# Cosine attention and a gated feed-forward on one core: the order of every engine through the third batch, rewritten

## The chip, the cores and the metric

The kernel runs on one core of one Trainium2 chip. The metric is the device time of one execution in microseconds. Before the change it is 416.95 us, the median of three runs (416.65, 416.95, 417.01).

## The reference, cut to what matters

```python
batch, n_heads, seq, head_dim = (8, 12, 448, 64)          # q, k, v
n_tokens, d_model, d_ff = (3584, 768, 2048)               # w_in, w_out

q_n = q / (np.linalg.norm(q, axis=-1, keepdims=True) + 1e-06)
k_n = k / (np.linalg.norm(k, axis=-1, keepdims=True) + 1e-06)
scores = np.matmul(q_n, k_n.transpose(0, 1, 3, 2)) / tau
attn = np.exp(scores - np.max(scores, axis=-1, keepdims=True))
attn = attn / (np.sum(attn, axis=-1, keepdims=True) + 1e-09)
x = np.matmul(attn, v)              # transposed and reshaped to 3584 x 768
h = x @ w_in
out = (h * np.cos(h)) @ w_out       # 3584 x 768, float32
```

## The kernel before, in words

**Units of work.** Four heads of one batch make a *quad*; there are three quads in a batch and 24 in all. A quad has seven score blocks. One block is four matmuls on TensorE (`scores`, L619), and an exp on ScalarE (L627, and L634 for quad 0) turns it into a tile of `E`. When the seven tiles of a quad are there, `attend` (L646) multiplies them with V. The row sums of `E` come in two ways: quads 0 to 5 use `spread` (L672), whose sums go through a Ln and an Exp of 128x896 elements on ScalarE (L685, L689); later quads use `sums` (L735), on two quads at a time, whose reciprocals are spread by DMA. The product of the two is `xT`.

**Normalization.** For each quad q and k are loaded (L452), squared (L505 on GpSimd or VectorE, L502 on ScalarE), summed (L509, VectorE), inverted by small ScalarE and VectorE instructions (L527 to L545), scaled (L553) and transposed, by TensorE in the first quads (L582, copied out at L590 or L592) and by a DMA later. Quad 0 is split into two pieces along the sequence, here called Q0a and Q0b, K0a and K0b. Its k is only cast (L561), and the scale of k goes into the exp.

**The feed-forward of a batch** has a stage `m1` (L784: eight pairs of blocks of `w_in`, 96 matmuls, with ScalarE L797 and L801 and VectorE L799 and L803 behind each pair) and a stage `m2` (L815: tiles of 128 tokens by 384 outputs, 16 matmuls each, copied out at L827 on VectorE, or on ScalarE where a table says so). Batches of 448 tokens give six, eight, six and eight such tiles in batches 0 to 3. The score blocks of later quads are put between the matmuls of `m2`. Three slots of two PSUM banks go round among score blocks, `spread` and `attend`, so a score block waits for the third one back to be read out. The exp and the sine need different ScalarE tables, so each stage starts with a table load (L424).

**What sets the order.** The kernel is an explicit program: a planner in Python orders the operations of each engine before the program is built, and each engine runs its list strictly in that order.

- The operations are numbered as the source issues them. Up to about number 210 (quads 0 to 2 and the norms of quads 3 and 4) a key, the number plus an entry of `MOVE`, sets the order on every engine's list, DMA issues among them. After that TensorE follows the source, DMA issues of GpSimd keep the order of their keys, and the planner's reckoned times order the rest.
- `VISITS` has a row for each batch: a pair (n, m) takes n entries off the stream of score blocks, spreads and attends, and then m matmuls of `m2`. `LATER` says how many score blocks of a quad go ahead of the attend of the quad before it.
- `ENG` puts single operations on an engine: `s0:16` is the square of q in quad 16 (`s1` of k), `n0` and `n1` the scaling, `x` the product of `attend` and reciprocal, `a` the copy of `attend` out of PSUM, `o:2:1` the copy-out of tile 2, half 1 of `m2`. Defaults are GpSimd for squares, scaling of q and `x`, and VectorE for the copies.
- `TREE` adds tiles of `E` on VectorE ahead of `sums`.
- 143 plus 70 products of the identity (L921, L925) stand in the list of TensorE as filling.

Loads of q and k and the DMA transposes are issued by SyncE (queue q1 of the profile), one piece of k by ScalarE (q10), and V, `w_in` (W1, L474) and `w_out` (W2, L479) by GpSimd (q0). W1(i, h) is half h of the partitions of the columns that `m1`'s pairs 4i to 4i+3 need; W2(i) holds four of the sixteen row blocks.

Numbers that the prediction names: 8 to 15 are the loads of quads 0 to 2, 65 and 66 of quad 3, 146 and 147 of quad 5; 17, 50, 53, 102 load V of quads 0 to 3; 51, 52, 54, 55 load W1(0,0), W1(0,1), W1(1,0), W1(1,1); 103 to 106 load W2(0) to W2(3). 33 squares K0b, 20 squares K0a, 39 and 23 are their sums, 30 is the last step of the inverse norm of Q0, 37 and 38 scale Q0.

Of the kernel before, what the change touches and what calls it, by code (L numbers as in the profile page):

```python
# [28 lines left out]
LATER = {18: -1, 5: 3, 7: -1, 21: -1, 9: 4, 10: -2, 12: 0, 23: 2, 15: -2, 13: -1, 22: 2, 8: 1, 16: 2, 14: 0, 17: -1,  # L29
    19: -1, 20: 0}  # L30
QUADS = [4, 5, 3, 3, 3, 3, 0, 0]
EARLY = [2, 1, 1, 1, 1, 1, 1, 1]
MOVE = {49: 2.0, 100: -6.5, 94: -4.0, 199: 5.5, 198: 3.0, 48: -155.0, 123: 23.0, 33: -18.5, 21: -15.0, 149: -9.5, 143:
# [17 lines left out]
TREE = {12: 3, 11: 0, 13: 0, 16: 4, 14: 6, 15: 6, 17: 4, 18: 2, 19: 0, 23: 6, 20: 6, 22: 5, 21: 6}  # L51
# [1156 lines left out]
```

## Time and profile before

| what | value |
|---|---|
| median of the runs | 416.95 us |
| the profiled execution, its own time | 417.37 us |
| its span, first to last instruction | 415.6 us |
| TensorE busy | 406.9 us (98%) |
| ScalarE busy | 313.7 us (75%) |
| VectorE busy | 306.6 us (74%) |
| GpSimd busy | 199.6 us (48%) |
| granted TensorE clock | 1.00 |

All times inside the execution are counted from the first instruction. PE is TensorE, ACT ScalarE, DVE VectorE, POOL GpSimd, SP SyncE. An instruction's busy time on PE begins before its predecessor's ends, so that the distance between two starts is what one costs.

### The profile page before, as it was taken

What the parts mean: (1) busy time and instruction counts of PE and PEld (TensorE: products, weight loads), DVE (VectorE), ACT (ScalarE), POOL (GpSimd) and SP (SyncE); (2) the same over time, 40 slices, a digit from 0 to 9 for tenths busy, and PEclk for the clock granted to TensorE, in tenths of its full rate; (3) what the DMA queues carried; (4) which work ended last, traced back from release to release, by engine and by line L of the source; (5) the groups of instructions that cost most, each with busy time, mean ns of one, the idle gap of its engine ahead of it and who ended that gap; (6) DMA issues with size and microseconds to landing.
All of it is one profiled execution on the core that took longest, in us unless ns stands there. A gap on an engine that the chain in (4) does not pass through costs nothing.

```text
span 415.6 us, 8581 instructions
## 1 busy us (share of the span) xinstructions
PE 406.9 (98%) x3600; PEld 217.5 (52%) x3601; DVE 306.6 (74%) x368; ACT 313.7 (75%) x417; POOL 199.6 (48%) x132
## 2 busy tenths in 40 slices
PE   7999999999999999999999999999999999999996
PEld 6674544445554455454555555454555555555563
DVE  4958997879853669963899899964988479836931
ACT  5998889988888987878878667889886667715700
POOL 3866329793386862688715495088504050030000
PEclk9999999999999999999999999999999999999999
DMA  8999999986099999199939689299803350071033
GB/s 267 231 244 209 236 225 275 217 180 152 4 205 168 262 236 237 40 177 244 188 113 176 132 181 219 33 162 211 178 2 82 77 108 22 1 165 39 0 77 76
DMA packets 71399, 62.83 MB, mean 151 GB/s; under 512 B 40512, under 2 KB 66240, under 8 KB 71360
## 3 DMA queue, kind: packets, MB, share of 16 engines
q1 hardware_dynamic: 60688, 50.09, 52.3%
q0 software_dynamic: 10240, 11.80, 17.6%
q8 instruction: 28, 0.46, 0.5%
q10 hardware_dynamic: 432, 0.39, 0.3%
q14 instruction: 11, 0.09, 0.1%
HBM read 45.61 MB, written 11.01 MB: 136 GB/s over the span
## 4 chain that ended last, share of the span: by engine, by line
PE 88%; ACT 8%; DVE 1%; DMA 1%; issue 0%; SPq 0%; DVEq 0%
PE PS L815 35%; PE PS L784 35%; PE PS L619 8%; PE PS L646 6%; ACT E L627 5%; PE PS L735 2%; PE PS L672 1%; DMA Kf<-in_k_dram 1%; ACT E L634 1%; ACT ar L689 1%; ACT ar L685 1%; PE PS L582 0%; DVE n L509 0%; DVE AVs L659 0%; DVE Qn L553 0%
## 5 line engine op out<-in xcount | busy, mean ns | idle before, releaser
L815 PE MATMUL PS<-W,gT 128*128 128x384 bf16 (+2 forms) x895 | 156.4, 327 | 0.1
L627 ACT ACTIVATE E<-PS 128x896 f16<-128x896 f32 x161 | 137.0, 917 | 21.8 <-PE PS L619 21.2
L784 PE MATMUL PS<-xT,W 128*128 128x448 bf16 x768 | 147.0, 352 | 0.0
L815 PEld LDWEIGHTS PS<-W,gT 128*128 128x128 bf16 x896 | 83.2, 98 | 69.1 <-issue 15.2
L784 PEld LDWEIGHTS PS<-xT,W 128*128 128x128 bf16 x768 | 74.7, 98 | 70.0 <-issue 0.4
L797 ACT ACTIVATE ar<-PS 128x896 int32<-128x896 f32 x64 | 58.2, 911 | 32.1 <-PE PS L784 31.4
L799 DVE SCALAR_TENSOR_TENSOR ar<-ar,PS 128x896 f32<-128x896 int32 x64 | 69.0, 1084 | 17.9 <-ACT ar L797 17.7
L803 DVE TENSOR_TENSOR gT<-PS,ar 128x896 bf16<-128x896 f32 x64 | 69.3, 1088 | 4.9 <-ACT ar L801 4.3
L801 ACT ACTIVATE ar<-ar 128x896 f32<-128x896 f32 x64 | 60.5, 947 | 16.0 <-DVE ar L799 15.3
L762 POOL TENSOR_TENSOR xT<-AVs,R 128x896 bf16<-128x896 f32 x17 | 37.9, 2231 | 57.4 <-DMA R<-Zs 57.4
L827 DVE COPY osb<-PS 128x384 f32<-128x384 f32 (+2 forms) x56 | 31.1, 554 | 41.6 <-PE PS L815 40.7
L505 POOL TENSOR_TENSOR sqq<-Qf 128x896 bf16<-128x896 f32 x21 | 35.3, 1680 | 44.4 <-DVE n L509 35.1
L619 PE MATMUL PS<-qT,kT 64*64 64x448 bf16 x672 | 51.0, 360 | 2.1 <-ACT E L627 1.2
L553 POOL TENSOR_TENSOR Qn<-Qf,rr 128x896 bf16<-128x896 f32 x20 | 37.9, 1897 | 29.7 <-DVE rr L545 25.7
L722 DVE TENSOR_TENSOR E<-E 128x1792 f16<-128x1792 f16 (+2 forms) x26 | 36.5, 1403 | 4.7 <-PE PS L646 4.5
L646 PE MATMUL PS<-E,Vb 64*64 64x448 f16 x672 | 37.7, 350 | 0.0
L505 POOL TENSOR_TENSOR sqk<-Kf 128x896 bf16<-128x896 f32 x17 | 30.5, 1797 | 13.6 <-DVE n L509 10.7
L553 POOL TENSOR_TENSOR Kn<-Kf,rr 128x896 bf16<-128x896 f32 x17 | 31.2, 1835 | 6.0 <-DVE Qn L553 3.6
L659 DVE COPY AVs<-PS 128x896 f32<-128x896 f32 x21 | 22.8, 1087 | 11.7 <-PE PS L646 11.5
L619 PEld LDWEIGHTS PS<-qT,kT 64*64 64x64 bf16 x672 | 16.3, 105 | 28.0 <-issue 11.3
L509 DVE TENSOR_REDUCE n<-sqq 128x14 f32<-128x896 bf16 (+2 forms) x23 | 23.7, 1035 | 6.8 <-POOL sqq L505 6.0
L646 PEld LDWEIGHTS PS<-E,Vb 64*64 64x64 bf16 x672 | 20.0, 107 | 11.8 <-ACT E L627 0.9
(57 smaller groups left out, 232.8 us busy)
## 6 DMA issues: line engine op xcount, KB each, us to landing
out_dram<-osb SPq DMA_DIRECT2D x54, 192.0 KB, 3.0
Qf<-in_q_dram SPq DMA_DIRECT2D x23, 448.0 KB, 5.1
Kf<-in_k_dram SPq DMA_DIRECT2D x23, 448.0 KB, 5.1
R<-Zs SPq DMA_DIRECT2D x72, 112.0 KB, 3.0
Vb<-in_v_dram POOLq DMA_DIRECT2D x24, 224.0 KB, 5.2
W<-in_moe_w_in_dram POOLq DMA_DIRECT2D x4, 768.0 KB, 17.3
W<-in_moe_w_out_dram POOLq DMA_DIRECT2D x4, 768.0 KB, 25.1
qT<-Qn SPq DMA_TRANSPOSE x20, 4.3
```

The lines of the kernel that those rows point to most:

```text
L505: op(eng, (1.68 if eng == "pool" else 1.05) * n, lambda e: e.tensor_tensor(dst, src, src, ALU.mult), r=cut(nm + "f", s, part), w=own, afte ...
L553: lambda e: e.tensor_tensor(n[0].ap()[:, j0:j1].rearrange("p j r d -> p r j d"), f[s].ap()[:, :, j0:j1], rb, ALU.mult),
L619: ins = e.matmul(bank(bs + r, S, 64 * a, 64 * a + 64), kT[u].ap()[64 * r:64 * r + 64, j, a, :], qT[u].ap()[64 * r:64 * r + 64, :, a, :], s ...
L627: act("exp", 0.81, lambda e: e.activation(E.ap()[:, es], two(bs), ACT.Exp, bias=SHIFT, scale=INV_TAU), r=pair(bs), w=[("E", es)], chain="E")
L646: ins = e.matmul(bank(bk + a, S, 64 * r, 64 * r + 64), Vb[vs].ap()[64 * a:64 * a + 64, r, j, :], E.ap()[64 * a:64 * a + 64, es, r, :], sta ...
L762: op(eng, 2.04 if eng == "pool" else 1.05, lambda e, u=u, sl=sl, b=b, c0=c0: e.tensor_tensor(xT[b % 2].ap()[:, c0:c0 + 2, :], AVs[sl].ap() ...
L784: ins = e.matmul(bank(bk + i2), W1.ap()[:, i, 128 * nb:128 * nb + 128], xT[c % 2].ap()[:, i, :], start=(i == 0), stop=(i == NKC - 1))
L797: op("act", 0.815, lambda e: e.activation(ar[s].ap().bitcast(I32), two(bk), ACT.Identity, bias=0.25, scale=INV2PI), r=bs, w=[("ar", s)], a ...
L799: op("dve", 1.005, lambda e: e.scalar_tensor_tensor(ar[s].ap(), ar[s].ap().bitcast(I32), -2.0 * math.pi, two(bk), ALU.mult, ALU.add), r=bs ...
L801: act("sin", 0.86, lambda e: e.activation(ar[s].ap(), ar[s].ap(), ACT.Sin, bias=GUARD * math.pi / 2.0, scale=GUARD), r=[("ar", s)], w=[("a ...
L803: op("dve", 1.01, lambda e: e.tensor_tensor(gT.ap()[:, 2 * pr:2 * pr + 2, col:col + S], two(bk), ar[s].ap(), ALU.mult), r=bs + [("ar", s)] ...
L815: ins = e.matmul(bank(bk, x1 - x0), gT.ap()[:, f, col:col + 128], W2.ap()[:, f, x0:x1], start=(f == 0), stop=(f == NNB - 1))
```

## The change

Only tables change. Rows 0 to 3 of `VISITS`, and `LATER` for quads 7 and 9, give another interleaving of score blocks and `m2`; the number of pieces and of changes between kinds of matmul stays nearly the same. `MOVE` is written anew for all operations from 7 to 210, so every list has a new order up to the first `m1`. In `ENG` nine copy-outs (`o`) and two `a` go from VectorE to ScalarE, the squares of q in quads 16 and 17 from GpSimd to ScalarE, and four steps (`s1:15`, `n0:16`, `x:10`, `x:13`) from GpSimd to VectorE; the other new entries name the engine that the default gives already. `TREE` of quad 12 becomes 0: three additions less on VectorE.

```diff
 VISITS = [
-    [(0, 25), (3, 12), (3, 11), (3, 3), (3, 5), (3, 12), (3, 10), (3, 4), (3, 4), (3, 0), (3, 4), (3, 5), (1, 1)],
-    [(0, 20), (3, 11), (3, 13), (3, 13), (3, 0), (3, 15), (3, 11), (3, 8), (6, 0), (3, 16), (2, 11), (4, 4), (2, 6),
-        (2, 0)],
-    [(0, 26), (2, 11), (3, 0), (2, 20), (4, 11), (3, 9), (2, 10), (5, 0), (3, 2)],
-    [(0, 21), (3, 9), (3, 11), (3, 8), (2, 8), (4, 26), (4, 17), (2, 12), (3, 11)],
+    [(0, 24), (3, 13), (3, 11), (2, 4), (7, 12), (3, 11), (3, 3), (3, 5), (1, 3), (6, 5), (2, 3), (1, 7)],
+    [(0, 24), (2, 0), (1, 8), (3, 14), (3, 7), (1, 3), (3, 0), (3, 19), (3, 7), (2, 10), (6, 0), (3, 16), (2, 12), (5,
+        4), (3, 7)],
+    [(0, 26), (2, 11), (3, 0), (2, 20), (4, 8), (3, 8), (2, 12), (5, 0), (3, 2)],
+    [(0, 19), (3, 11), (3, 13), (3, 6), (2, 9), (4, 27), (5, 16), (1, 11), (3, 11)],
...
-LATER = {18: -1, 5: 3, 7: -1, 21: -1, 9: 4, 10: -2, 12: 0, 23: 2, 15: -2, 13: -1, 22: 2, 8: 1, 16: 2, 14: 0, 17: -1,
-    19: -1, 20: 0}
+LATER = {18: -1, 5: 3, 7: 0, 21: -1, 9: 5, 10: -2, 12: 0, 23: 2, 15: -2, 13: -1, 22: 2, 8: 1, 16: 2, 14: 0, 17: -1,
+    19: -1, 20: 0, 3: 0, 4: 0, 11: 0}
...
-MOVE = {49: 2.0, 100: -6.5, 94: -4.0, 199: 5.5, 198: 3.0, 48: -155.0, 123: 23.0, 33: -18.5, 21: -15.0, 149: -9.5, 143:
...
+MOVE = {7: -2.38, 8: -8.0, 9: -5.4, 10: -2.8, 11: -11.0, 12: -1.2, 13: 1.4, 14: 31.581, 15: 6.21, 16: 19.154, 17:
+    25.294, 18: 3.48, 19: 10.468, 20: 14.944, 21: 4.754, 22: 11.03, 23: 16.217, 24: 17.411, 25: 18.979, 26: 16.779,
+    27: 11.389, 28: 11.997, 29: 12.605, 30: 13.213, 31: 12.933, 32: 13.541, 33: -0.798, 34: 17.841, 35: 18.449, 36:
+    10.261, 37: 11.707, 38: 8.007, 39: -3.107, 40: 13.147, 41: 14.715, 42: 9.689, 43: 10.915, 44: 0.653, 45: 9.169,
+    46: 9.777, 47: 39.345, 48: -29.13, 49: 3.307, 50: -48.2, 51: 11.387, 52: 14.527, 53: 17.667, 54: 61.079, 55:
+    51.199, 56: 2.583, 57: 4.043, 58: 1.783, 59: 7.263, 60: -10.417, 61: 8.983, 62: -4.257, 63: -34.404, 64: -0.137,
+    65: -11.283, 66: -24.019, 67: 2.281, 68: 5.811, 69: -7.459, 70: 6.385, 71: -5.355, 72: -0.517, 73: 0.091, 74:
...
+    94: -8.921, 95: -8.511, 96: -3.211, 97: -4.781, 98: -3.213, 99: 3.461, 100: 1.459, 101: -9.621, 102: 39.761, 103:
+    -1.541, 104: 6.339, 105: 14.219, 106: 17.959, 107: -5.739, 108: 4.811, 109: -10.463, 110: -2.241, 111: 4.505, 112:
...
+    139: 0.949, 140: 3.543, 141: 5.099, 142: 7.477, 143: -0.099, 144: 1.361, 145: 1.777, 146: 84.142, 147: 86.742,
...
 ENG = {'s1:13': 'act', 's1:21': 'act', 's1:22': 'act', 's1:23': 'act', 'o:3:1': 'dve', 'n1:12': 'dve', 'o:5:1': 'dve',
     's0:15': 'pool', 's1:14': 'pool', 's0:20': 'pool', 'o:14:0': 'dve', 'o:16:1': 'dve', 'n0:20': 'pool', 'n1:19':
-    'pool'}
-TREE = {12: 3, 11: 0, 13: 0, 16: 4, 14: 6, 15: 6, 17: 4, 18: 2, 19: 0, 23: 6, 20: 6, 22: 5, 21: 6}
+    'pool', 'o:2:0': 'act', 'x:9': 'pool', 's1:15': 'dve', 'o:10:0': 'act', 'o:7:0': 'act', 'x:6': 'pool', 'o:3:0':
+    'act', 's0:9': 'pool', 's1:9': 'pool', 'x:10': 'dve', 's0:17': 'act', 's0:16': 'act', 'n0:11': 'pool', 'o:7:1':
+    'act', 'n1:14': 'pool', 's1:17': 'pool', 'n0:13': 'pool', 'o:2:1': 'act', 'o:9:0': 'act', 'o:9:1': 'act', 's1:16':
+    'pool', 'x:11': 'pool', 'x:12': 'pool', 's0:11': 'pool', 'a:11': 'act', 'x:13': 'dve', 'a:14': 'act', 'o:5:0':
+    'act', 'n0:16': 'dve', 'a:4': 'dve', 'o:8:1': 'dve', 'a:13': 'dve'}
+TREE = {12: 0, 11: 0, 13: 0, 16: 4, 14: 6, 15: 6, 17: 4, 18: 2, 19: 0, 23: 6, 20: 6, 22: 5, 21: 6}
```

24 rows, old and new, of the table MOVE are left out of this document.

## The prediction

> **What bounds the kernel now.** I read the page's head first, then the table of stages, then the chain of waits and the timelines of single engines inside the stages that the change rewrites, and last the DMA queues. The head of the page and two of the groups of instructions:
>
> ```profile
> span 415.6 us, 8581 instructions
> PE 406.9 (98%) x3600; PEld 217.5 (52%) x3601; DVE 306.6 (74%) x368; ACT 313.7 (75%) x417; POOL 199.6 (48%) x132
> ...
> L921 PE MATMUL PS<-ident 128*128 128x128 bf16 x143 | 11.7, 252 | 1.5 <-DVE ident L405 1.4
> ...
> L925 PE MATMUL PS<-ident 64*64 64x128 bf16 x70 | 3.0, 218 | 0.0
> ```
>
> TensorE is busy for all but 8.7 us, and 14.7 us of its busy time (11.7 + 3.0) is filling that the change neither adds nor removes. An order alone can therefore save little: it must take away waits that hide inside the busy time, or shorten the start, where filling covers a wait for others. The table of stages cuts the span at the first exp, the first `m1`, the first score block of batch 0, the second `m1`, and `m2` of batch 1. Columns are length, busy time and instructions of PE, weight loads, DVE, ACT and POOL, granted clock, DMA share and GB/s:
>
> ```profile
> 11.12:35.11 23.99, 22.19 (x406) 15.15 (x402) 17.89 (x27) 23.34 (x39) 18.10 (x18) 1.00 1.11 234
> 35.11:58.35 23.24, 23.24 (x139) 12.38 (x135) 21.36 (x25) 19.88 (x25) 9.35 (x7) 1.00 1.18 218
> 58.35:87.25 28.90, 28.47 (x353) 13.53 (x353) 23.35 (x29) 28.41 (x42) 21.92 (x13) 1.00 0.99 229
> ...
> 105.60:145.80 40.20, 39.99 (x465) 19.86 (x464) 24.88 (x35) 36.17 (x53) 27.74 (x19) 1.00 0.83 167
> ```
>
> So the stage up to 35.11 is ScalarE's (23.34 of 23.99 us busy), the stage 58.35 to 87.25 is ScalarE's and TensorE's together, and behind that TensorE works alone with ScalarE 4.0 us free in batch 1. The DMA engines are full until the end of batch 0. The clock is 1.00 throughout, so clock plays no part.
>
> **The change part by part: the start.** ScalarE's and VectorE's timelines ahead of the first exp, and one piece of the chain:
>
> ```profile
> 1.75 4.74 DMA Kf<-in_k_dram
> 6.51 0.63 ACT L502 ACTIVATE sqk<-Kf 128x512 bf16<-128x512 f32 x1 [0.65 <-DMA Kf<-in_k_dram]
> 7.53 0.21 ACT L534 ACTIVATE nrm<-nrm 128x14 f32<-128x14 f32 x1
> 8.25 0.20 ACT L536 ACTIVATE rr<-nrm 128x14 f32<-128x14 f32 x1
> 11.12 2.21 ACT L634 ACTIVATE E<-PS,rr 128x448 f16<-128x448 f32 x4 [1.25 <-PE PS L619]
> 7.17 1.15 DVE L509 TENSOR_REDUCE n<-sqk 128x8 f32<-128x512 bf16 x2 [0.55 <-ACT sqk L502]
> 8.57 1.15 DVE L553 TENSOR_TENSOR Qn<-Qf,rr 128x384 bf16<-128x384 f32 x2
> ```
>
> Everything hangs on K0a, which lands at 6.49 (1.75 + 4.74): its square, then both sums of K0 (23, then 39) in 1.15 us of VectorE, then the copy of kT, then the scaling of Q0 at 8.57. The new order puts sum 39, whose input does not need K0a, ahead of 23. It fits into VectorE's wait of 0.55 us. Six of the 14 columns leave the path: 1.15 x 6/14 = 0.49 us. The other input of the scaling, the last inverse step (30), moves ahead of two small ones and would start at about 7.78, right behind the instruction at 7.53, so it is not late next: 8.57 - 0.49 = 8.08 still leaves it 0.1 us. Term: -0.5 us (bounds -0.5 and 0), because ScalarE is without slack from the first exp to `m1` and hands an earlier start on.
>
> At the other end of this stage the small Ln of quad 3 (196) now stands between the last Ln and the last Exp of the row sums. Such a small one costs 0.25 us from start to start:
>
> ```profile
> 36.84 0.21 ACT L527 ACTIVATE nrm<-n 128x28 f32<-128x28 f32 x1
> 37.09 0.23 ACT L539 ACTIVATE ne<-nrm 128x28 f32<-128x28 f32 x1
> ```
>
> Term: +0.2 us (0 to 0.25). The rest of this stage's new order I cost at nothing: ScalarE runs the same exps back to back, and filling covers TensorE.
>
> **The loads in front.** V of quad 1 (50) was issued behind V of quad 0, which waits for q of quad 1; now it is GpSimd's first DMA, with nothing to wait for, in the middle of Q0 and K0. In exchange q of quad 2 (14) goes behind k of quad 3 (66), which waits for the readers of K0, one of them the square that ends at 7.14, so one load leaves the early stretch. The size of a load of V, and the queues in three windows (packets, MB, share of 16 engines), in the order 10.5 to 12.5, 21.5 to 23.5 and 43.6 to 47 us, with SyncE's issue ahead of the last:
>
> ```profile
> Vb<-in_v_dram POOLq DMA_DIRECT2D x24, 224.0 KB, 5.2
> ...
> q0 software_dynamic: 467, 0.40, 124.7%
> q1 hardware_dynamic: 5, 0.01, 1.0%
> ...
> q0 software_dynamic: 130, 0.27, 70.3%
> q1 hardware_dynamic: 130, 0.23, 36.4%
> ...
> 43.57 0.37 SPq L452 DMA_DIRECT2D Qf<-in_q_dram  x1
> ...
> q0 software_dynamic: 481, 0.71, 116.0%
> ```
>
> V of one quad is 224 KB, 0.23 MB; at 0.40 MB in 2.0 us it fills the engines for 1.15 us. If it moves packet for packet with Q0 and K0, K0a lands up to 1.15 us later; if it queues behind what was issued first, K0a loses nothing. The trace shows both: 130 packets against 130 in the second window, but none of q1 in the 3.4 us after an issue at 43.57 in the third. Since V's issue comes after Q0a's and before K0a's, I take +0.3 us, nearer to the window in which the newcomer waits (bounds 0 and 1.15).
>
> The Trainium skill, DMA: Bandwidth & Descriptors, section on queues, rings and completion order, states that each DMA engine takes turns between the queues that have work, packet by packet. By that rule the term would be 1.15 us and the sum -0.15 us; the second window agrees with it, and the third doesn't show it at once.
>
> **W1 behind W2.** GpSimd's list was W1(0,0), W1(0,1), V, W1(1,0), W1(1,1), W2(0), W2(1) and so on; now W2(0) stands ahead of W1(1,1), and W2(1) ahead of W1(1,0). What that does to the second half of the first `m1`:
>
> ```profile
> L474 POOL DMA_DIRECT2D W<-in_moe_w_in_dram x4: 669/692/726, 11.2 to 14.0; - x4
> ...
> DMA to landing us min/median/max: 9.9/17.3/22.7
> ...
> 43.84 10.38 PE L784 MATMUL PS<-xT,W 128*128 128x448 bf16 x54
> ```
>
> The last W1 piece landed at 14.0 + 22.7 = 36.7. W2(1) had landed at 43.57, when SyncE could issue the load of quad 5 that waits for it. The queue is served in order, so W1(1,0), now in that place, lands at about 43.6. TensorE needs it at pair 4: 42 of 96 matmuls are done at 43.84, and six more of 10.38/54 = 0.19 us end at 45.0. It arrives 1.4 us ahead: cost nothing, and the cover is those 1.4 us. One place further back it would be (43.57 - 36.7)/2 = 3.4 us later, at 47.0, and TensorE would wait 2.0 us. The load of quad 5, issued earlier now, pushes that way, but a newcomer waited 3.4 us above.
>
> **The visits.** Pieces of the chain in batches 0 and 1, TensorE's timeline at its worst stops, the VectorE copy that one waits for, and the nearest row to a copy-out on ScalarE:
>
> ```profile
> 58.42 0.69 PE PS L619 x12
> 72.04 0.89 PE PS L619 x12
> 84.98 0.93 PE PS L619 x12
> ...
> 79.78 0.99 PE L619 MATMUL PS<-qT,kT 64*64 64x448 bf16 x12
> 81.19 1.52 PE L672 MATMUL PS<-E,ones 64*64 64x448 f16 x28 [0.42 <-ACT E L627]
> ...
> 121.68 0.54 ACT L750 ACTIVATE Zs<-PS 128x448 f32<-128x448 f32 x1 [0.85 <-PE PS L735]
> ...
> 138.13 0.50 PE PS L619 x8
> 142.76 1.09 DVE AVs L659
> 143.29 0.38 PE L619 MATMUL PS<-qT,kT 64*64 64x448 bf16 x4
> 143.89 0.38 PE L619 MATMUL PS<-qT,kT 64*64 64x448 bf16 x4 [0.21 <-DVE AVs L659]
> 144.20 1.15 PE L815 MATMUL PS<-W,gT 128*128 128x384 bf16 x6
> ...
> 188.10 0.87 PE L619 MATMUL PS<-qT,kT 64*64 64x448 bf16 x8
> 188.90 1.51 PE L735 MATMUL PS<-E,sel 128*32 128x448 f16 x22
> ```
>
> Three score blocks cost 0.69 us when nothing holds them; in batch 0 they cost up to 0.93, and 1.41 at 79.78. The stops sum to 0.20 + 0.24 + 0.72 = 1.2 us, but ScalarE was idle for only 0.49 us of that stage (28.90 - 28.41), and the exps are the same ones. The new row starts its first score block one matmul earlier. Two copy-outs (`o:2:0`, `o:2:1`) come onto ScalarE, some 0.54 us each; nobody waits for them before the next `m1` needs their banks, so I put them behind the exps, in `m1`, where ScalarE is not full. Term: -0.3 us, between -0.5 (all idle time gone; -1.2 if exps also move past the last score block) and +1.1 (both copies ahead of exps).
>
> In batch 1 two score blocks behind the copy of quad 10 took 144.20 - 143.29 = 0.91 us against 0.50, because the VectorE list had other work ahead of that copy. With a copy-out less on VectorE that is -0.4 us (0 to -0.4). The same kind at 188.10 costs 0.80 against 0.50, and quad 14's copy and the squares change engine: -0.3 us (0.3 either way). The moved steps from GpSimd to VectorE lie in stages where VectorE is free for a quarter of the time.
>
> **Sum:** -0.5 + 0.2 + 0.3 - 0.3 - 0.4 - 0.3 = -1.0 us on the profiled execution's 417.37, or 416.4. That execution is 0.42 us above the median of 416.95, so the forecast as a median is 415.95.
>
> **The rivals.** *V in front takes turns with K0a* (no change): the V term is 1.15, the sum -0.15, and the time 416.8. For it is the second window, against it the third. *W1(1,0) a place late* (slower): the queue lags by another 3.4 us, TensorE stands 2.0 us before pair 4; -1.0 + 2.0 gives 417.95. It decides as soon as W1(1,0) lands after 45.0; the 1.4 us of cover speak against it. *ScalarE becomes the bound of batch 1* (slower): two copy-outs (1.1 us) and a new interleaving come onto an engine with 4.0 us of idle time there. If its exps fall behind as in batch 0, each of 14 visits costs some 0.2 us (0.89 against 0.69), 2.8 us, and the -0.4 of that batch is not had either: -1.0 + 0.4 + 2.8 = +2.2, or 419.15. It decides once ScalarE's idle time in the stage is gone; 4.0 against 1.1 us speaks against it, the strictly fixed lists speak for it.
>
> **How the numbers follow.** A difference of 0.2% (0.83 us) is about what a measurement of this kernel can tell from no change. The forecast, with its better variants, has 0.44; V taking turns 0.22; W1 late 0.12; ScalarE as the bound of batch 1 0.22. If the exps also move past batch 0's last score block (-1.2 for -0.3) and V costs nothing, the sum is -2.2, or 414.75; a little below that is the low end. The high end is the last rival's 419.15. Faster 0.44, same 0.22, slower 0.34. The forecast's own range is 414.5 to 416.5.
>
> **What would show it.** Right: K0a lands within 0.3 us of 6.5; the scaling of Q0 starts 0.2 us or more earlier than 8.57 and the first exp before 11.1; `m1` begins by 35.1 with no stop at pair 4; batch 0 takes at most 28.7 us; two score blocks behind quad 10's attend cost about 0.5 us. Wrong: ScalarE's square of K0a later than 7; a gap in L784 near 45; ScalarE over 39 us busy in batch 1 with score blocks at 0.9 us. All the steps could hold and the forecast still fail, if a stop appears in batches 4 and 5, whose tables stay but whose start shifts.

## The result: slower by 1.25%, and the profile after

The changed kernel takes 422.01 us (median of six runs, 419.68 to 423.96); the kernel before, beside it, takes 416.92 (416.65 to 417.38). The ratio is 1.0125, 95% interval 1.009 to 1.0159. The forecast of 415.95 was wrong in sign, and the result lies beyond 419.15, the high end of the range. The runs also scatter over 4.3 us, where those of the kernel before lie within 0.7.

The profiled execution took 423.69 us. The head of its page, and the shares by engine in the chain of work that ended last, first of the kernel after, then of the kernel before (lines of the source are 15 higher in the changed kernel, so L784 is L799, L619 is L634, L598 is L613):

```profile
span 421.9 us, 8591 instructions
PE 407.9 (97%) x3606; PEld 216.4 (51%) x3607; DVE 300.0 (71%) x360; ACT 319.7 (76%) x430; POOL 185.7 (44%) x126
PE 69%; ACT 11%; DMA 9%; issue 4%; POOL 3%; DVE 2%; SPq 1%; ACTq 0%; POOLq 0%
```

```profile
PE 88%; ACT 8%; DVE 1%; DMA 1%; issue 0%; SPq 0%; DVEq 0%
```

No engine has more work to speak of. What is new is that DMA, issue and GpSimd stand on the chain with 16% together, where DMA had 1%. The table of stages, in the order first exp to `m1`, `m1` of batch 0, batch 0, then from one `m1` to the next for batches 1 to 3; columns as in the prediction:

```profile
12.00:36.77 24.77, 22.32 (x397) 13.27 (x393) 17.89 (x27) 23.57 (x38) 17.35 (x18) 1.00 1.12 232
36.77:59.89 23.12, 23.12 (x142) 12.32 (x141) 21.23 (x24) 19.55 (x25) 9.18 (x7) 1.00 1.19 214
59.89:88.89 29.00, 28.18 (x353) 13.41 (x353) 22.45 (x28) 28.37 (x42) 22.05 (x13) 1.00 1.00 214
...
107.22:148.33 41.11, 40.24 (x465) 19.75 (x463) 22.93 (x31) 36.62 (x54) 27.72 (x19) 1.00 0.82 155
148.33:198.26 49.93, 46.76 (x418) 24.00 (x416) 34.14 (x40) 40.61 (x56) 24.70 (x16) 1.00 0.87 190
198.26:247.95 49.69, 49.51 (x399) 25.71 (x397) 40.91 (x46) 40.44 (x54) 22.16 (x14) 1.00 0.69 144
```

The same two last stages of the kernel before:

```profile
145.79:192.51 46.72, 46.59 (x415) 23.64 (x411) 33.08 (x41) 37.91 (x50) 28.68 (x17) 1.00 0.84 177
192.51:241.62 49.11, 49.11 (x398) 25.57 (x398) 41.94 (x46) 38.55 (x50) 27.66 (x18) 1.00 0.80 166
```

`m1` of batch 0 begins 1.67 us late (36.77 against 35.11). Batch 1 costs 0.91 more, the next stage 3.21 (49.93 - 46.72), batch 3 0.58, and from there on the two executions run 6.33 us apart to the end. Four places hold 5.4 us of that. The first is the start. K0a lands at 7.83 in place of 6.49; ScalarE's timeline shows its square, the first exps, and one stop more on the way to `m1`:

```profile
7.85 0.63 ACT L517 ACTIVATE sqk<-Kf 128x512 bf16<-128x512 f32 x1 [1.95 <-DMA Kf<-in_k_dram]
12.00 2.21 ACT L649 ACTIVATE E<-PS,rr 128x448 f16<-128x448 f32 x4 [0.79 <-PE PS L634]
20.61 0.92 ACT L700 ACTIVATE ar<-PS 128x896 f32<-128x896 f32 x1 [0.49 <-PE PS L687]
```

The other three are TensorE's waits between 107 and 200 us, where the kernel before has one of 0.2; behind the first two stand SyncE's issues around quad 14 and quad 10, which the second fence shows in order of time:

```profile
PE PS L634 <- issue: 2.4, 1, 2.4
PE PS L634 <- DMA kT<-Kn: 0.7, 1, 0.7
PE PS L799 <- DVE xT L777: 0.6, 1, 0.6
```

```profile
122.18 1.24 SPq L613 DMA_TRANSPOSE qT<-Qn  x1
124.79 5.45 SPq L773 DMA_DIRECT2D R<-Zs  x8
130.29 1.37 SPq L613 DMA_TRANSPOSE kT<-Kn  x1
...
178.48 1.25 SPq L613 DMA_TRANSPOSE qT<-Qn  x1
179.77 5.22 SPq L773 DMA_DIRECT2D R<-Zs  x8
185.03 1.47 SPq L613 DMA_TRANSPOSE kT<-Kn  x1
```

The DMA view from 185 to 186 us, with the time from issue to landing, and TensorE's timeline where it goes on:

```profile
Vb<-in_v_dram POOLq DMA_DIRECT2D x1, 224.0 KB, 4.9
kT<-Kn SPq DMA_TRANSPOSE x1, 6.7
```

```profile
191.81 0.57 PE L634 MATMUL PS<-qT,kT 64*64 64x448 bf16 x8 [2.41 <-issue]
```

For two quads whose row sums are inverted together, SyncE issues eight spreads of the reciprocals (R), 5.2 to 5.5 us in a row. In the new list they stand between the transposes of q and k of one quad. The transpose of k of quad 14 is issued at 185.03 and takes 6.7 us, so it lands at 191.7, and the first score block of quad 14 starts at 191.81. The wait is called "issue" there; the landing beside it names what ended it. SyncE's timeline of the kernel before, around quad 10 and around quad 14, and the time from issue to landing of the last transpose shown:

```profile
122.99 1.40 SPq L598 DMA_TRANSPOSE kT<-Kn  x1
124.44 5.29 SPq L758 DMA_DIRECT2D R<-Zs  x8
...
175.41 5.20 SPq L758 DMA_DIRECT2D R<-Zs  x8
180.66 1.41 SPq L598 DMA_TRANSPOSE qT<-Qn  x1
182.11 1.60 SPq L598 DMA_TRANSPOSE kT<-Kn  x1
...
kT<-Kn SPq DMA_TRANSPOSE x1, 3.5
```

The two stops are of different kinds. At quad 10 the transpose of k stood ahead of the spreads and now stands behind them. Counted from the first `m1` matmul of its batch it was issued at 35.7 us and is now issued at 41.4; it landed at 39.3, 6.2 us ahead of its score block, and lands now at 46.6, where the score block waits for it. At quad 14 the spreads stand in front of the transpose of k in both lists, and it is issued hardly later: 36.3 us into its stage before, 36.7 now. What grew is the time to its landing, from 3.5 to 6.7 us. Before, it landed at 185.6, 0.8 us ahead of the score block at 186.38, so there was no room for that. The DMA view has one thing near it that is new at this place: a load of V on GpSimd's queue (the line `Vb` above), issued at 184.79, 0.24 us ahead of the transpose. In the kernel before the only load of V in this stage goes out 43.2 us into it, behind the landing.

### The profile page after: what moved, and what is told of

Same layout as the page of the kernel before. It is cut to its first block, busy times and chain, and to the rows that moved or that the text cites. A ratio compares the mean times of both kernels' runs of the same rounds, so it can differ in the third digit from the quotient of the medians.

```text
span 421.9 us, 8591 instructions
## 1 busy us (share of the span) xinstructions
PE 407.9 (97%) x3606; PEld 216.4 (51%) x3607; DVE 300.0 (71%) x360; ACT 319.7 (76%) x430; POOL 185.7 (44%) x126
## 4 chain that ended last, share of the span: by engine, by line
PE 69%; ACT 11%; DMA 9%; issue 4%; POOL 3%; DVE 2%; SPq 1%; ACTq 0%; POOLq 0%
PE PS L799 30%; PE PS L830 28%; ACT E L642 7%; PE PS L634 5%; PE PS L661 4%; DMA kT<-Kn 3%; DMA qT<-Qn 2%; DMA R<-Zs 2%; ACT E L649 2%; POOL Qn L568 1%; PE PS L750 1%; DMA Kf<-in_k_dram 1%; DMA Qf<-in_q_dram 1%; PE PS L687 1%; DVE AVs L674 1%
## 5 line engine op out<-in xcount | busy, mean ns | idle before, releaser
L799 PE MATMUL PS<-xT,W 128*128 128x448 bf16 x768 | 147.2, 353 | 0.6 <-DVE xT L777 0.6
L799 PEld LDWEIGHTS PS<-xT,W 128*128 128x128 bf16 x768 | 74.7, 98 | 70.9 <-DVE xT L777 1.1
L777 POOL TENSOR_TENSOR xT<-AVs,R 128x896 bf16<-128x896 f32 x15 | 34.4, 2293 | 59.4 <-DMA R<-Zs 59.3
L634 PE MATMUL PS<-qT,kT 64*64 64x448 bf16 x672 | 51.1, 361 | 6.9 <-issue 2.4
L842 DVE COPY osb<-PS 128x384 f32<-128x384 f32 (+2 forms) x47 | 26.0, 554 | 39.5 <-PE PS L830 38.7
L568 POOL TENSOR_TENSOR Qn<-Qf,rr 128x896 bf16<-128x896 f32 x19 | 35.4, 1864 | 36.0 <-DVE rr L560 32.7
L520 POOL TENSOR_TENSOR sqq<-Qf 128x896 bf16<-128x896 f32 x19 | 31.8, 1675 | 39.2 <-DVE n L524 36.4
L737 DVE TENSOR_TENSOR E<-E 128x1792 f16<-128x1792 f16 (+2 forms) x25 | 32.0, 1280 | 6.7 <-PE PS L661 6.4
L634 PEld LDWEIGHTS PS<-qT,kT 64*64 64x64 bf16 x672 | 16.3, 105 | 35.4 <-issue 14.0
L568 POOL TENSOR_TENSOR Kn<-Kf,rr 128x896 bf16<-128x896 f32 x17 | 29.0, 1707 | 11.2 <-DMA kT<-Kn 6.6
L674 DVE COPY AVs<-PS 128x896 f32<-128x896 f32 x19 | 20.7, 1087 | 17.5 <-PE PS L661 17.3
L520 POOL TENSOR_TENSOR sqk<-Kf 128x896 bf16<-128x896 f32 x16 | 28.5, 1778 | 10.1 <-DVE n L524 5.3
L479 POOL DMA_DIRECT2D Vb<-in_v_dram x24 | 18.0, 753 | 29.2 <-PE PS L634 25.0
```

Source lines behind the costliest of these rows:

```text
L520: op(eng, (1.68 if eng == "pool" else 1.05) * n, lambda e: e.tensor_tensor(dst, src, src, ALU.mult), r=cut(nm + "f", s, part), w=own, afte ...
L568: lambda e: e.tensor_tensor(n[0].ap()[:, j0:j1].rearrange("p j r d -> p r j d"), f[s].ap()[:, :, j0:j1], rb, ALU.mult),
L634: ins = e.matmul(bank(bs + r, S, 64 * a, 64 * a + 64), kT[u].ap()[64 * r:64 * r + 64, j, a, :], qT[u].ap()[64 * r:64 * r + 64, :, a, :], s ...
L777: op(eng, 2.04 if eng == "pool" else 1.05, lambda e, u=u, sl=sl, b=b, c0=c0: e.tensor_tensor(xT[b % 2].ap()[:, c0:c0 + 2, :], AVs[sl].ap() ...
L799: ins = e.matmul(bank(bk + i2), W1.ap()[:, i, 128 * nb:128 * nb + 128], xT[c % 2].ap()[:, i, :], start=(i == 0), stop=(i == NKC - 1))
```

## The experiments

Each kernel takes finished lists and moves entries in them; all waits are worked out anew. In the diffs `ahead` and `behind` move one entry, and `head` and `tail` cut a list where both kernels have had the same operations on that engine (107 entries of TensorE's, into `m2` of batch 0; 114 of ScalarE's, 84 of VectorE's, 47 of GpSimd's and 42 of SyncE's, near the end of batch 0). Ratios are to the kernel before in the same session. The table at the end of this section sets the stages of all runs side by side.

**The load of V in front, and the two transposes.**

```diff
 # v1_back: the changed kernel
+behind("pool", V[1], V[0])
 # kt_ahead: the changed kernel
+ahead("sp", KT[quad 10], first of its eight R); ahead("sp", KT[quad 14], first of its eight R)
 # v1_kt: both.   v1_front: the kernel before
+ahead("pool", V[1], first operation of the list behind the iota)
```

> The kernel after, with the load of V of quad 1 put back behind that of quad 0 in GpSimd's list; every other list is unchanged. Theory (front load): V takes turns with Q0 and K0, which made K0a land at 7.83 instead of 6.49; here K0a lands at 6.5, the first exp starts at about 10.7 (the sum order saves 0.4 against before's 11.12) and m1 at about 35.4, 1.3 earlier than 36.77; the later stops stay, so the total is about 420.7 against 422.0. Rival (the newcomer waits; K0a was late for another reason, such as the load of k of quad 2 in front of q): K0a stays near 7.8 and the total at 422. Rival (the later stops only follow from the late start): they vanish too, and the total is about 417.

> The kernel after, with SyncE's transposes of k of quads 10 and 14 put ahead of the eight DMAs each that spread reciprocals. Theory (held transposes): the transposes are issued about 4 us earlier, the first score blocks of quads 10 and 14 don't wait for them, and of the 4.7 us lost between the second and the fourth m1 some 3 go: about 419. The start is as in the kernel after (m1 at 36.8). Rival (new visits or the engines of the copies and scalings are what costs): the two waits move elsewhere and the total stays within 1 us of 422.

> The kernel after with both edits: V of quad 1 behind that of quad 0, and the transposes of k of quads 10 and 14 ahead of the spreads. If both theories hold and add up: about 422.0 - 1.3 - 3 = 417.7, the remaining 0.8 to before being the rest of the start and of batch 1. Rival (visits or engines): above 420.

> The kernel before with one edit: V of quad 1 is GpSimd's first DMA, as in the kernel after. Front load: K0a lands at about 7.8, the first exp is about 1.3 late, 12.4, m1 starts 1.0 to 1.3 late, and the total is about 418.0 (416.9 + 1.1), with the later stages shifted but without the stops of the kernel after. Rival (the newcomer waits): K0a near 6.5 and the total at 416.9. Rival (a late start alone sets off the later stops): above 420.

| kernel | median, us | from, to | ratio | 95% interval |
|---|---|---|---|---|
| v1_back | 420.72 | 419.86, 421.26 | 1.0085 | 1.0068 to 1.0101 |
| kt_ahead | 421.79 | 419.81, 423.31 | 1.0124 | 1.0096 to 1.0153 |
| v1_kt | 420.30 | 419.42, 421.12 | 1.0076 | 1.0058 to 1.0094 |
| v1_front | 417.73 | 416.60, 419.89 | 1.0013 | 0.9985 to 1.004 |

What V in front costs differs from one execution to the next. In the profiled one of v1_front K0a landed at 8.08, and `m1` of batch 0 began 2.45 us late; the batches behind it lost no more than 0.14. Not all of the 2.45 is the landing. For 3.41 us around the first score block the granted clock was 0.50 (third number from the end of the row):

```profile
10.90:14.31 3.41, 3.41 (x42) 2.37 (x41) 2.97 (x5) 1.35 (x6) 3.17 (x4) 0.50 0.91 197
```

From K0a to the first exp this execution took 5.41 us, 0.6 to 0.8 more than the others with the old start (4.63 to 4.81). In the execution of kt_ahead, with the same load in front, K0a landed at 6.02. With V back the scatter of the changed kernel falls from 4.3 to 1.4 us (four runs against six), and the median by 1.3, though the intervals of the ratios still overlap. With the old batches a late start does not set off later stops (v1_front), and with the new ones they come without it (start_old below).

Moving both transposes gained nothing in the time. The stop at quad 14 went (batch 2 costs what it did before), but batch 1 became 1.9 to 2.2 us longer. ScalarE's and GpSimd's timelines of v1_kt show why:

```profile
140.36 0.23 ACT L587 ACTIVATE nrm<-n 128x28 f32<-128x28 f32 x1 [1.99 <-DVE n L569]
...
133.82 2.10 POOL L822 TENSOR_TENSOR xT<-AVs,R 128x896 bf16<-128x896 f32 x1 [1.65 <-DMA R<-Zs]
135.88 1.69 POOL L613 TENSOR_TENSOR Kn<-Kf,rr 128x896 bf16<-128x896 f32 x1
137.53 1.68 POOL L565 TENSOR_TENSOR sqk<-Kf 128x896 bf16<-128x896 f32 x1
```

With the transpose of quad 10 first, the eight spreads come later. GpSimd, whose new list has the products of quads 6 and 7 ahead of quad 11's scaling, waits 1.65 us for them; so the square and the sum of quad 12 are late, and the small logarithm that needs them stands in ScalarE's list ahead of exps that are ready.

**Which half: start or batches.**

```diff
 # start_new: lists[e] = head(changed, e) + tail(before, e), then
+behind("pool", V[1], V[0])
 # start_ln0: start_new
+behind("act", Ln[quad 0], E[8])
 # start_old: lists[e] = head(before, e) + tail(changed, e)
 # r_behind: the changed kernel with V[1] back and
+lists["sp"] = head(changed, "sp") + tail(before, "sp"); ahead("pool", Kn[quad 11], x[quad 6])
```

> The kernel before from the end of batch 0 on, and ahead of that point the changed kernel's lists of every engine, with V of quad 1 put back behind V of quad 0. If the loss lies in the lists of batches 1 to 3 (the theory), this keeps what the new start gains when V is out of the way (m1 of batch 1 was 0.29 us earlier in the run with V back and the k transposes ahead): 416.7 us. If the new start does harm that shows only later (the rival), most of the 3.2 us that are left stays: 419 or more.

> As start_new, with one operation of ScalarE moved: the logarithm of quad 0's spread sum behind the two exponentials (into E7 and E8) that the changed kernel put it ahead of. The first exponential starts 0.9 to 1.1 us earlier than before in the runs with V back, but only 0.3 of that is left at m1 of batch 0; ScalarE stood 0.49 us ahead of this logarithm. If that place costs what was lost, 0.5 less than start_new: 416.2 us. If the gain is lost elsewhere, as start_new.

> The other half: the changed kernel from the end of batch 0 on, and ahead of it the lists of the kernel before, so V of quad 1 too where it was. Theory (lists of batches 1 to 3): 3 us slower than before, 420. Rival (the start): as before, 417.

> The changed kernel with V of quad 1 back, SyncE's list from batch 1 on as before (the sixteen-row spreads of reciprocals behind the k transposes of quads 10 and ahead of both of quad 14), and on GpSimd the scaling of k of quad 11 ahead of the two x products of quads 6 and 7 again, as before. Theory: the stops at score blocks 10 and 14 and the stop of ScalarE at the logarithm of quad 12 go, which cost about 2 us of the 3.7 of the run with V back alone; the loss of 0.6 in batch 3 stays: 418. Rival: the transposes were only the first of several late inputs, and other lists (VectorE's and ScalarE's copies, the visits) hold the time: 420 or more.

| kernel | median, us | from, to | ratio | 95% interval |
|---|---|---|---|---|
| start_new | 417.49 | 417.04, 420.52 | 1.0008 | 0.9987 to 1.0029 |
| start_ln0 | 416.86 | 416.10, 418.92 | 0.999 | 0.997 to 1.0009 |
| start_old | 420.90 | 420.41, 422.62 | 1.0088 | 1.0064 to 1.0113 |
| r_behind | 420.80 | 419.30, 424.82 | 1.0102 | 1.0063 to 1.0142 |

This settles the half: with the old start and the new batches the whole loss behind the front load is there (1.0088, as v1_back's 1.0085); with the new start and the old batches there is none. In start_old's execution batch 1 cost nothing and batch 2 4.17 us, with this wait of TensorE between 165 and 195, and SyncE's issues of quad 14 in the same order as after; below them the time to landing of the transpose of k and of the load of V issued just ahead of it, and the row of the clock behind the wait:

```profile
PE PS L762 <- issue: 3.0, 1, 3.0
```

```profile
174.99 1.24 SPq L741 DMA_TRANSPOSE qT<-Qn  x1
176.27 5.22 SPq L901 DMA_DIRECT2D R<-Zs  x8
181.54 1.52 SPq L741 DMA_TRANSPOSE kT<-Kn  x1
...
Vb<-in_v_dram POOLq DMA_DIRECT2D x1, 224.0 KB, 5.5
kT<-Kn SPq DMA_TRANSPOSE x1, 7.3
...
188.62:192.03 3.41, 3.12 (x36) 1.88 (x40) 0.00 (x0) 1.73 (x2) 1.69 (x1) 0.50 1.08 369
```

The transpose is issued 35.9 us into the stage here, 0.5 earlier than in the kernel before, and still comes too late. So it goes in v1_back: issued at 35.9 with the load of V 0.28 us ahead of it, landed after 6.0 us, a wait of 1.8. In the 16 other executions, where no load of V goes out in the 4 us ahead of it, this transpose lands after 2.9 to 3.7 us. TensorE waited 1.2 us longer than in v1_back, and the stage took 2.4 us longer; 3.41 us at half clock, with TensorE busy for 3.12 of them, are enough for the rest.

r_behind, meant as the repair, failed. The stop at quad 14 went again (batch 2: +0.12), but ScalarE's logarithm of quad 12 still waited 1.1 us in batch 1, and batch 3 cost 1.46.

The start's gain is not in the total. From the first exp to `m1` the lists of before took 23.97 to 24.13 us in six executions and the new ones 24.77 to 25.15 in nine; with the logarithm moved (here and in three kernels below) it was 24.28, 24.31, 24.63 and 25.04. So the new order behind the first exp costs some 0.8 us, and that logarithm's place seems to be a part of it.

The profiled execution of start_ln0 is the slowest of its twelve (418.92), and shows a stop that the prediction had as a rival. TensorE's only wait between 35 and 60 us:

```profile
PE PS L911 <- DMA W<-in_moe_w_in_dram: 1.7, 1, 1.7
```

W1(1,0) landed at 47.05 there. In the nine other executions with it behind W2(1) it landed between 43.1 and 46.3; where it came at 46.3, in v1_kt14 below, TensorE stood 0.4 us for it.

**One list at a time.**

```diff
 # sp_new: the kernel before
+lists["sp"] = head(before, "sp") + tail(changed, "sp")
 # visits_new: the kernel before, the other four lists kept
+VISITS[1:4], LATER = those of the change
 # rest_new: the changed kernel, V[1] back, the other three lists kept
+VISITS[1:4], LATER = those before; lists["sp"] = head(changed, "sp") + tail(before, "sp")
 # start_w: start_ln0
+behind("pool", W1[1,0], W1[1,1])
```

> The kernel before with one engine's list changed: SyncE's from batch 1 on in the changed kernel's order, so the eight spreads of reciprocals ahead of the transpose of k of quad 10 and between the transposes of quad 14. If that order by itself sets off the stops at score blocks 10 and 14 (the theory), about 2 us slower, 419.2, most of it at block 14. If it hurts only where the other engines' lists bring the spreads or k late (the rival), within 0.5 of the kernel before.

> The kernel before with TensorE's list changed alone: rows 1 to 3 of VISITS and the table LATER of the changed kernel, the four other engines' lists as they were. The loss of 0.57 us in batch 3 came in every run with the changed rows, without one long stop: if it belongs to the row, it is here too, 417.8. If the rows also take the cover from score blocks 6 to 11 (blocks of quad 6 started 0.5 to 0.6 us later in all runs with the new rows), 418.5 or more.

> The changed kernel with V of quad 1 back, and with SyncE's list from batch 1 on and TensorE's rows 1 to 3 of VISITS as before: what is left new there are the lists of ScalarE, VectorE and GpSimd with the copies and products that changed engines. If SyncE and the rows carry the loss, 417.5. If these three lists carry it, 419.5 or more.

> The kernel before from the end of batch 0 on; ahead of it the changed lists with three repairs: V of quad 1 behind V of quad 0, ScalarE's logarithm of quad 0's sums behind the exponentials into E7 and E8, and the last part of W1 directly behind the other part of its half, ahead of the second part of W2. In the profiled execution of the kernel without the third repair that part of W1 landed at 47.05 us and TensorE stood 1.7 us for it; here it should land by 43. Expected 0.5 under the kernel before and free of that stop: 416.6.

| kernel | median, us | from, to | ratio | 95% interval |
|---|---|---|---|---|
| sp_new | 431.28 | 430.56, 432.86 | 1.0332 | 1.0301 to 1.0364 |
| visits_new | 419.24 | 419.15, 423.87 | 1.0059 | 1.0018 to 1.01 |
| rest_new | 429.02 | 426.86, 432.22 | 1.0279 | 1.0235 to 1.0323 |
| start_w | 417.23 | 416.36, 418.48 | 0.9995 | 0.998 to 1.001 |

The first three say little about the parts and much about the whole: sp_new and rest_new lose 14 and 12 us, more than all new lists together (5), and visits_new 2. In sp_new TensorE waits 3.4 us for a product `x` on VectorE in `m1` of batch 2, a stop of 0.6 us in the kernel after and of nothing in the kernel before. A part of the two great losses is the clock: it was 0.50 for 6.8 us in the profiled execution of each, and all eight runs of the two have a mean clock of 0.987 to 0.996. One thing sp_new does settle. It has the spreads between the two transposes of quad 14, as after, but GpSimd's old list, and no load of V near:

```profile
187.12 5.19 SPq L799 DMA_DIRECT2D R<-Zs  x8
192.36 1.37 SPq L639 DMA_TRANSPOSE kT<-Kn  x1
...
kT<-Kn SPq DMA_TRANSPOSE x1, 3.6
```

Spreads right in front of the transpose do not by themselves make its landing long. That the load of V does is likely, and not shown: no run moves that load alone.

Neither "SyncE's list" nor "the visits" carries the loss as a sum of parts would have it. start_w removed the stop for W1 (it landed at 41.65) and gained nothing that the runs can tell.

**Repairs one by one.**

```diff
 # v1_kt14: the changed kernel, V[1] back and
+ahead("sp", KT[quad 14], first of its eight R)
 # v1_kt14_r3: v1_kt14
+VISITS[3] = the row before
 # repaired: v1_kt14_r3
+behind("act", Ln[quad 0], E[8]); behind("pool", W1[1,0], W1[1,1])
 # repaired2: repaired
+behind("sp", KT[quad 10], fourth of its eight R); copy "a:14" back in VectorE's list
 # sum_first: the kernel before
+ahead("dve", sum 39, sum 23); ahead("act", step 30, Ln of K0a); ahead("act", Ln of K0b, second step of K0a)
```

> The changed kernel with two repairs: V of quad 1 back behind V of quad 0, and on SyncE the transpose of k of quad 14 ahead of the eight spreads in front of it (that of quad 10 stays where the change put it, since moving it took the stop to quad 12's logarithm, 1.9 us in batch 1). Theory: batch 1 costs 0.03 as with V back alone, batch 2 nothing as with both transposes moved, batch 3 its 0.57, so 0.6 above the kernel before: 417.8. Rival: every repair of one stop brings the next, and it stays at 420.

> The same with row 3 of VISITS as before; the other engines' lists stay. Theory: the 0.57 of batch 3 goes as well, as the kernel before: 417.2. Rival: 0.57 belongs to the other lists and stays, as the run without it.

> The same with two repairs of the start more: the logarithm of quad 0's sums behind the exponentials into E7 and E8, and the last part of W1 ahead of the second part of W2. If the start's saving of up to 0.8 us at the first exponential were kept, 416.6; the run with these two repairs on the old lists showed 0.14 of it at m1 of batch 0 and no difference in the median, so by that as the run without them.

> The repaired kernel with two changes more for what its profile still shows over the kernel before: the transpose of k of quad 10 in the middle of the eight spreads in front of it (behind the four for quad 6), for 0.4 us at score block 10, and the copy of quad 14's attend sums on VectorE again, as before, for the 0.66 us that ScalarE lags in batch 3. If those two are all that is left, 417.1, as the kernel before, less what of the start's 0.6 is kept: down to 416.6. If one of them only moves the stop, 418 or more.

> The kernel before with only the change's order of the first sums: on VectorE the sum over the second part of k of quad 0 ahead of the one over its first part, on ScalarE the last inverse step of q ahead of the logarithms of k. This is the prediction's first term alone: first exponential 0.46 us earlier, and, if ScalarE hands it on as the prediction had it, 416.7 us. If the start gives it back before m1 of batch 0, as the runs with the whole new start did, no difference: 417.15.

| kernel | median, us | from, to | ratio | 95% interval |
|---|---|---|---|---|
| v1_kt14 | 419.09 | 417.55, 421.01 | 1.0041 | 1.0021 to 1.0061 |
| v1_kt14_r3 | 418.75 | 417.80, 421.77 | 1.0043 | 1.002 to 1.0066 |
| repaired | 418.14 | 417.58, 419.51 | 1.0021 | 1.0004 to 1.0038 |
| repaired2 | 421.20 | 420.16, 422.20 | 1.0085 | 1.0057 to 1.0113 |
| sum_first | 416.86 | 416.41, 417.93 | 0.9984 | 0.9956 to 1.0012 |

The place of one transpose is worth 0.4%: v1_back 1.0085, v1_kt14 1.0041, and the intervals do not touch. Ahead of the spreads the transpose of k of quad 14 goes out 31.0 us into the stage in place of 35.9, also ahead of that load of V, and lands after 3.0. Row 3 of `VISITS` is worth nothing by itself: batch 3 stays 0.66 us long without it, and visits_new has 0.51 with it on the old lists, so either half of the change there costs what both cost. Of what is left in the repaired kernel, the profile shows a wait for the transpose of k of quad 10 (TensorE's only one between 125 and 145 us) and a longer batch 3 (49.77 against 49.11, row of the table of stages):

```profile
PE PS L724 <- DMA kT<-Kn: 0.7, 1, 0.7
```

```profile
192.67:242.44 49.77, 49.44 (x398) 25.55 (x397) 40.28 (x46) 40.37 (x54) 23.31 (x15) 1.00 0.71 154
```

Going after both made it worse: in repaired2 the same small logarithm of quad 12 stops ScalarE again, and batch 3 costs 1.26:

```profile
141.64 0.23 ACT L632 ACTIVATE nrm<-n 128x28 f32<-128x28 f32 x1 [2.42 <-DVE n L614]
```

So the transpose of quad 10 and the products of quads 6 and 7 are tied: give way to one and the other stops. What makes up the last 0.2% of the repaired kernel was not settled, and no version here beats the kernel before by more than its interval.

K0a's landing, the wait from there to the first exp, and the difference of each stage to the kernel before (from one first `m1` matmul to the next, in TensorE's timeline; one execution each):

| kernel | K0a | to first exp | to `m1` 0 | batch 0 | batch 1 | batch 2 | batch 3 |
|---|---|---|---|---|---|---|---|
| before | 6.49 | 4.63 | 35.11 | 52.14 | 58.54 | 46.72 | 49.11 |
| after | 7.83 | 4.17 | +1.67 | -0.02 | +0.90 | +3.21 | +0.58 |
| v1_back | 5.94 | 4.28 | +0.13 | +0.09 | +0.03 | +1.76 | +0.57 |
| kt_ahead | 6.02 | 4.17 | -0.12 | +0.01 | +2.15 | -0.08 | +0.57 |
| v1_kt | 5.71 | 4.30 | -0.30 | +0.02 | +1.91 | -0.08 | +0.57 |
| v1_front | 8.08 | 5.41 | +2.45 | +0.03 | +0.14 | 0.00 | 0.00 |
| start_new | 6.57 | 4.17 | +0.78 | +0.02 | -0.34 | 0.00 | 0.00 |
| start_ln0 | 6.91 | 4.18 | +0.26 | +1.72 | -0.34 | 0.00 | 0.00 |
| start_old | 5.92 | 4.78 | -0.28 | +0.13 | +0.03 | +4.17 | +0.57 |
| r_behind | 5.72 | 4.93 | +0.33 | +0.01 | +1.03 | +0.12 | +1.46 |
| sp_new | 5.73 | 4.78 | -0.63 | +0.03 | +4.61 | +5.70 | +4.13 |
| visits_new | 5.72 | 4.81 | -0.59 | +0.02 | +1.95 | -0.01 | +0.51 |
| rest_new | 6.75 | 4.18 | +0.61 | +0.02 | +7.39 | +0.60 | +2.93 |
| start_w | 6.15 | 4.18 | -0.14 | +0.03 | -0.01 | 0.00 | 0.00 |
| v1_kt14 | 6.87 | 4.17 | +0.85 | +0.46 | +1.10 | -0.08 | +1.41 |
| v1_kt14_r3 | 5.71 | 4.81 | +0.20 | +0.01 | +0.03 | -0.08 | +0.66 |
| repaired | 5.79 | 4.37 | -0.64 | +0.01 | +0.88 | -0.08 | +0.66 |
| repaired2 | 6.45 | 4.18 | +0.55 | +0.01 | +2.34 | -0.08 | +1.26 |
| sum_first | 5.79 | 4.79 | -0.56 | +0.02 | -0.03 | 0.00 | 0.00 |

Two things stand in it. The old lists of batches 2 and 3 take the same time to 0.01 us, whatever the start brought them (from -0.56 to +2.45). The new ones differ from one execution to the next: with the same lists of batch 1 in six executions it costs 0.03 three times (v1_back, start_old, v1_kt14_r3), and 0.88, 0.90 and 1.10 (repaired, after, v1_kt14). The landing of the transpose of k of quad 10 parts them. It is issued 41.2 to 41.4 us into the batch in all six. In the first three it landed after 3.7 to 4.1 us, ahead of the score block, which is ready for it at 45.8; in the others after 5.2 to 5.5 us, behind that. No load of V is near it, and why it took longer there stays open.

## Why the prediction was wrong, point by point

**The step that failed most is one that the prediction did not take:** the lists behind batch 0. It priced the visits and the copies of batches 1 to 3 at -0.7 together, from the stops that the kernel before had, and weighed no queue that the new order moves a step past. SyncE's list was not read at all, nor the time that the transposes take to land. At quad 10 the new list puts eight spreads (5.5 us) in front of a transpose that had 6.2 us to spare, so that its landing decides whether TensorE waits. At quad 14 a transpose with 0.8 us to spare is issued within 0.5 us of its old time and takes 2.5 to 3.8 us longer to land, each time with a load of V issued just ahead of it. Measured: +4.7 us in batches 1 to 3 of the profiled execution, about 3.6 in the medians (420.90 of start_old against 417.29). The stop at quad 14 is shown to be the late landing of that transpose, since issuing it 5 us earlier removed the stop and 0.4% of the time; what lengthens the landing is open.

**The sum ahead of the other (-0.5).** Right in its mechanism, of less worth than thought. From K0a to the first exp the new order takes 4.17 us where the old took 4.63, so 0.46 less. But that is so only where K0a lands late. With K0a at 5.71 to 5.79 the first exp starts at 10.51 and 10.53 in the old order and between 10.02 and 10.65 in the new one. sum_first, which is this step alone, cannot be told from no change. Its chain, and below it that of visits_new with the old order, shows why (K0a at 5.79 and 5.72):

```profile
5.58 2.20 DVE n L580 x4
...
5.53 2.20 DVE n L598 x4
```

VectorE makes all four sums back to back there, and has no wait for K0a in which one of them could be hidden.

**V in front (+0.3, bounds 0 and 1.15).** Mis-sized. K0a landed 1.34 us later than in the profile before, 1.59 in v1_front, and 0.47 earlier in kt_ahead; without V in front it landed anywhere from 5.71 to 6.91. The upper bound took the transfer of V as the most that it could cost, and one landing of K0a, 6.49, as that of the kernel. The rival "takes turns" had the better end for this term. The Trainium skill (DMA: Bandwidth & Descriptors, section on queues, rings and completion order) has each DMA engine take turns between the queues that have work. Two of three executions have a delay as that would give; the third, where K0a landed at 6.02, does not show it.

**The rest of the start, at nothing; the logarithm of quad 3, +0.2.** Both wrong. The stage from the first exp to `m1` became 0.78 us longer. The logarithm of quad 3 has no part in it, since `m1` begins at 36.77, ahead of it at 37.52. The prediction looked at the small one that it had a price for, and not at the large one of quad 0, moved past two exps. That this one carries the 0.78 is not shown: with it moved back, one execution in four still took 25.04.

**W1 behind W2.** Right for the profiled execution: forecast to land at 43.6, it landed at 44.07 and TensorE didn't wait. But of ten executions with this order one had it at 47.05, which cost 1.7, and one at 46.31, which cost 0.4. The mechanism, price and point of that rival were right; the cover of 1.4 us was thinner than one trace could show.

**The visits of batch 0 (-0.3).** Nothing came of it: 29.00 us against 28.90, with ScalarE again the bound at 28.37.

**Batch 1 (-0.4) and ScalarE as its bound.** The two score blocks behind quad 10's attend take 145.97 - 145.17 = 0.80 us, not 0.5; the gain was 0.1. The rival was wrong too: ScalarE is busy for 36.62 us of 41.11, so it has 4.5 us free, more than before. TensorE's rows behind that attend, in the timeline of after:

```profile
145.17 0.87 PE L634 MATMUL PS<-qT,kT 64*64 64x448 bf16 x8
145.97 0.82 PE L830 MATMUL PS<-W,gT 128*128 128x384 bf16 x4
```

**Batch 2 (-0.3).** The two score blocks behind quad 14's attend take 194.33 - 193.51 = 0.82 us, and 0.80 before, so nothing was gained there either:

```profile
193.51 0.89 PE L634 MATMUL PS<-qT,kT 64*64 64x448 bf16 x8
194.33 1.51 PE L750 MATMUL PS<-E,sel 128*32 128x448 f16 x28
```

The chances went with these terms: 0.34 for slower came from two stops, W1 and ScalarE's share, that are not what happened.

## What to carry to other kernels

An order that is fixed in advance has to be read for what stands in front of each transfer on its queue, with the spare time of the one that waits. Issue and landing have to be compared each by itself, counted from the start of the stage: at quad 14 the list made the transpose look held up by 5.2 us of spreads, and it was issued at its old time and landed late. A new list is good only with its partners, so a change of this kind is tried whole or cut where both versions have done the same work; exchanging one engine's list cost up to 14 us. And a time that one profile gives for a landing is one draw: before a load is moved in front of another, look at several executions.

## What the runs showed of the hardware

The same list gives different landings. K0a, the fourth load of the kernel, landed between 5.71 and 6.91 us in 16 executions without V in front of it, issued at 1.75 or 1.76 in all of them; W1(1,0) between 43.1 and 47.05. This is as large as the whole effect that the change aimed at. The old start hands it on: with K0a at 5.72 (visits_new) `m1` of batch 0 began at 34.52, with K0a at 6.49 (before) at 35.11. Nothing in these runs shows why the landings differ.

Transposes with a load of V just ahead landed later. Of the transposes of k issued behind 90 us in the nineteen traces, the 29 with a load of V issued in the 0.6 us ahead landed after 4.8 to 7.3 us (median 5.2), the 227 with no load of V under way after 2.9 to 6.6 (median 4.0). The ranges overlap, and the transfers beside them differ too, so this is no proof of the cause.

A long wait of TensorE cost more than its length. The granted clock is 1.00 in fifteen of the nineteen traces from its first record, at 4 to 7 us, up to the last microsecond. In the other four it falls to 0.50, for 3.41 us or twice that, and these four alone have waits of 2.9 us or more: 3.0 us up to 188.91 in start_old and 0.50 from 188.62 to 192.03; 2.9 us up to 147.65 in rest_new and 0.50 from 148.29 to 155.12; 3.2 us up to 8.80 in v1_front and 0.50 from 10.90 to 14.31; 3.4 us up to 154.86 in sp_new and 0.50 from 154.90 to 158.31. sp_new has one such stretch more, from 144.66, behind a wait of 1.5 us; the wait of 2.4 us in the kernel after had none behind it.
